# An FFT-and-maxout kernel: the first loads in one run, the table angles in two passes, and 35 table matmuls ahead of the work

## The chip, the cores and the metric

The kernel runs on one core of a Trainium2 chip. The metric is the device time of one execution in microseconds (us), the median of several runs. A core has a matrix engine (TensorE, PE in the profile; its weight loads are shown apart as PEld), three engines that work on vectors (VectorE or DVE, ScalarE or ACT, GpSimd or POOL) and SyncE (SP), which only issues transfers. Each works off its own list of instructions in the written order and waits on semaphores for the others. Transfers (DMAs) are issued by SyncE, ScalarE and GpSimd and carried out by 16 DMA engines that all share.

## The reference

```python
def _attn_ref(x):                      # x: 8 x 3072 x 256
    X = np.fft.fft(x, axis=1)
    X = np.fft.fft(X, axis=2)
    return X.real.astype(np.float32)

def _moe_ref(x, w1, w2, w3, w_out):    # x: 24576 x 256, d_ff = 768
    h = np.maximum(np.maximum(x @ w1, x @ w2), x @ w3)
    return (h @ w_out).astype(np.float32)
```

The output of the first goes into the second: the real part of a two-dimensional Fourier transform of each batch, then three projections, their maximum, and a projection back.

## The kernel before, in words

The transform along the sequence (3072 = 24 x 128) is done in two stages with matrices of sines and cosines, and the transform along the feature axis is folded into the weights, once, on the chip. The eight batches follow each other. A batch has two mixing stages: seven groups `s` (lines 421 to 442), small matmuls with the 24-point matrices `m24f`, `m24r`, `m0f`, `m0r`, whose results go to `z`; and six groups `k` (lines 444 to 462), which multiply `z` with the rows of the table `tab` into `t`. Then come 18 units of the feed-forward part (lines 470 to 502), into which the mixing of the next batch is woven by a plan written out by hand (lines 666 to 705). The schedule is manual: on each engine the instructions run in the order in which the program writes them.

The change lies in what happens before the first unit. That part consists of:

- Loads of batch 0. Rows 112 to 127 go to `xs_a` by SyncE and ScalarE (lines 165 and 166). The other 112 rows go to `x0_first` by sixteen transfers that GpSimd issues (lines 174, 182, 186, 187, all recorded at line 100), four for each run of 32 rows and four for the last 16. Between them GpSimd writes small index vectors: `i13` (line 172), `jm24` and `g24` (175 to 181), `dvec` (183 to 185). Behind them it issues the weight loads (191 to 198).
- The table. `tab` has 13 rows of 128 angles in three versions: sine, cosine and minus sine. `tab_angles` (233) takes three VectorE operations over all elements of the rows: angle in turns, rounding, remainder. `tab_sines` (246) takes three ScalarE passes: sine, absolute value, sine with a shift of a quarter turn (`half_pi`). `tab_minus` (254) is one VectorE operation. Rows 0 to 6 come first, then rows 7 to 12.
- The 24-point matrices (lines 262 to 302): some twenty small VectorE operations, one sine on ScalarE (292), and products on both.
- The rows of batch 0, turned and laid out: `turn_rows` and `lay_rows` (309 to 329, 346 to 355) copy each loaded run from (row, feature) into two arrays with the features outside, one of them reversed, on VectorE (`on_dve`) and ScalarE (`on_act`). The last strip is rows 95 to 111, split between the two engines by features.
- `md` and `nmd`, the 256-point matrix in two halves and its negative (lines 331 to 350): VectorE computes the angles `vm`, ScalarE takes the sine (345), VectorE derives the other half by alternating signs (349) and the negative (350). They multiply the weights in `prep_first` (367), which gives `gE`, `gO`, `gD`.
- The table matmuls (line 627), 27 matmuls on the finished table into a bank that nobody reads. They stand on TensorE ahead of the first `s` group.

Of the kernel before, what the change touches and what calls it, by code (L numbers as in the profile page):

```python
# [33 lines left out]
def kernel(  # L34
# [9 lines left out]
    nc = tc.nc  # L44
# [15 lines left out]
    consts = ctx.enter_context(tc.tile_pool(name="consts", bufs=1))  # L60
# [23 lines left out]
    gw = consts.tile([128, 768], BF16, tag="gw")  # L84
    rows_m = consts.tile([128, 12 * B], INT32, tag="rows_m")
    mark = consts.tile([1, 1], FP32, tag="mark")
    sgn = consts.tile([128, 1], FP32, tag="sgn")
    dif = consts.tile([128, 1], FP32, tag="dif")
    t_mid = consts.tile([128, 2, B], BF16, tag="t_mid")
# [6 lines left out]
    def load_rows(engs, dst, b, r0, r1, after=None):  # L96
        xr = x_rows(b)
        for g in range(4):
            eng = engs[g] if isinstance(engs, tuple) else engs
            ld = eng.dma_start(out=dst[g * 24:(g + 1) * 24], in_=xr[g, :, r0:r1, :])  # L100
            if after is not None:
                tc.add_manual_dep(ld.ins, after.ins.name, AFTER, reason="weights first")
# [50 lines left out]
    gen = gen_pool_cm.__enter__()  # L153
# [3 lines left out]
    def iota(t, pattern, base=0, cm=0):  # L157
        nc.gpsimd.iota(t, pattern, base=base, channel_multiplier=cm,
                       allow_small_or_imprecise_dtypes=True)
# [17 lines left out]
    iota(jm24[:, 13:24], [[-1, 11]], base=-1)  # L177
    iota(jm24[:, 24:37], [[1, 13]])
    iota(jm24[:, 37:48], [[1, 11]], base=1)
    g24 = gen.tile([96, 5], FP32, tag="g24")  # L180
    iota(g24, [[24, 5]])
    load_rows(nc.gpsimd, x0v[:, 32:64, :], 0, 32, 64)
    dvec = gen.tile([128, 128], FP32, tag="dvec")
    iota(dvec.rearrange("p (dl g) -> p dl g", g=4), [[1, 32], [64, 4]])
    iota(dvec[:, 2:4], [[64, 2]], base=32)
# [22 lines left out]
    nc.gpsimd.tensor_copy(rows_m, rows_f)  # L208

    consts_of = {}  # L210
    for (name, value) in (("half_pi", 0.5 * math.pi), ("rnd", ROUND), ("n24", -24.0)):
# [6 lines left out]
    half = gen.tile([128, 256], FP32, tag="half")  # L218
    nc.vector.memset(half[:, 0:128], 64.0)
    nc.vector.memset(half[:, 128:256], 0.0)  # L220
# [4 lines left out]
    nc.vector.tensor_scalar(out=pi13, in0=i13, scalar1=pidx, scalar2=1.0 / 3072.0,  # L225
                            op0=ALU.mult, op1=ALU.mult)

    w = gen.tile([128, 13 * 128], FP32, tag="w")
    v = gen.tile([128, 13 * 128], FP32, tag="v")
    q = gen.tile([128, 13 * 128], FP32, tag="q")  # L230
    turn = 2.0 * math.pi

    def tab_angles(r0, r1):
        cs = slice(r0 * 128, r1 * 128)
        n = r1 - r0
        nc.vector.scalar_tensor_tensor(
            out=v[:, cs].rearrange("p (r j) -> p r j", j=128),
            in0=j128.unsqueeze(1).to_broadcast([128, n, 128]), scalar=p128,
            in1=pi13[:, r0:r1].unsqueeze(2).to_broadcast([128, n, 128]),
            op0=ALU.mult, op1=ALU.add)  # L240
        nc.vector.tensor_scalar(out=q[:, cs], in0=v[:, cs], scalar1=ROUND, scalar2=None,
                                op0=ALU.add)
        nc.vector.scalar_tensor_tensor(out=w[:, cs], in0=q[:, cs], scalar=-ROUND, in1=v[:, cs],
                                       op0=ALU.add, op1=ALU.subtract)

    def tab_sines(r0, r1):
        cs = slice(r0 * 128, r1 * 128)
        wr = w[:, cs].rearrange("p (r j) -> p r j", j=128)
        nc.scalar.activation(out=tabs[:, r0:r1, 0, :], in_=wr, func=AX.Sin, scale=-turn)
        nc.scalar.activation(out=w[:, cs], in_=w[:, cs], func=AX.Abs)  # L250
        nc.scalar.activation(out=tabs[:, r0:r1, 1, :], in_=wr, func=AX.Sin, scale=-turn,
                             bias=consts_of["half_pi"])

    def tab_minus(r0, r1):
        nc.vector.tensor_scalar(out=tabs[:, r0:r1, 2, :], in0=tabs[:, r0:r1, 0, :],
                                scalar1=-1.0, scalar2=None, op0=ALU.mult)
# [52 lines left out]
    def turn_rows(copy, r0, n, d0, d1):  # L309
        reverse(copy, xr0, x0_first[:, r0 * 64:(r0 + n) * 64], r0, n, d0, d1)  # L310
# [4 lines left out]
    def lay_rows(copy, xs, r0, n, d0=0, d1=33):  # L315
        copy(out=xn0[:, d0:d1, r0:r0 + n],
             in_=bass.AP(xs.tensor, xs.offset + d0, [xs.ap[0], [1, d1 - d0], [64, n]]))

    def bf_rows(r0, n):
        return x0_first[:, r0 * 64:(r0 + n) * 64]  # L320
# [10 lines left out]
    turns = gen.tile([128, 256], BF16, tag="turns")  # L331
    nc.vector.memset(turns, 1.0)
    nc.vector.memset(turns.rearrange("p (q two g) -> p q two g", two=2, g=4)[:, :, 1, :], -1.0)
    vm = gen.tile([128, 256], FP32, tag="vm")
    qm = gen.tile([128, 256], FP32, tag="qm")
    nc.vector.scalar_tensor_tensor(
        out=vm.rearrange("p (k c) -> p k c", c=128),
        in0=dvec.unsqueeze(1).to_broadcast([128, 2, 128]), scalar=pidx,
        in1=half.rearrange("p (k c) -> p k c", c=128), op0=ALU.mult, op1=ALU.add)
    nc.vector.tensor_scalar(out=vm[:, 128:129], in0=pidx, scalar1=128.0, scalar2=64.0,  # L340
                            op0=ALU.mult, op1=ALU.add)
    nc.vector.tensor_scalar(out=qm, in0=vm, scalar1=256.0 * ROUND, scalar2=None, op0=ALU.add)
    nc.vector.scalar_tensor_tensor(out=vm, in0=qm, scalar=-256.0 * ROUND, in1=vm,
                                   op0=ALU.add, op1=ALU.subtract)
    nc.scalar.activation(out=md[0], in_=vm, func=AX.Sin, scale=float(-2.0 * math.pi / 256.0))
    turn_rows(on_act, 63, 32, 54, 65)
    turn_rows(on_dve, 63, 32, 32, 54)
    lay_rows(on_dve, bf_rows(64, 32), 64, 32)
    nc.vector.tensor_tensor(out=md[1], in0=md[0], in1=turns, op=ALU.mult)
    nc.vector.tensor_scalar(out=nmd_all, in0=md_all, scalar1=-1.0, scalar2=None, op0=ALU.mult)  # L350
    for (copy, a, b, c) in ((on_act, 49, 64, 17), (on_dve, 32, 49, 0)):
        turn_rows(copy, 95, 17, a, b)
        if copy is on_act:
            turn_rows(copy, 95, 16, 64, 65)
        lay_rows(copy, bf_rows(96, 16), 96, 16, c, c + 17 - c // 17)
    tab_minus(7, 13)
    nc.vector.tensor_scalar(out=sgn, in0=pidx, scalar1=0.0, scalar2=None, op0=ALU.is_equal)
    nc.vector.tensor_scalar(out=sgn, in0=sgn, scalar1=2.0, scalar2=-1.0,
                            op0=ALU.mult, op1=ALU.add)
# [263 lines left out]
                l2_queue.pop(0)  # L623

    warm = ps_s.tile([128, 512], FP32, name="warm", tag="ps")
    for _ in range(27):
        nc.tensor.matmul(warm, tab[:, 0:128], tab[:, 0:512], start=True, stop=True)
# [153 lines left out]
```

## Time and profile before

| | us |
|---|---|
| median of 3 runs | 425.91 (425.56 to 426.27) |
| the profiled execution | 424.57 |
| its span, first to last instruction | 422.8 |
| TensorE busy in the span | 404.0 (96%) |
| VectorE, ScalarE, GpSimd busy | 276.8, 258.9, 243.8 |

The profile is of one execution; its times are counted from the start of the span. The span plus 1.8 us around it is the execution's own time. In the rows of a list of instructions the first two numbers are start and length, then engine, line, operation, output, inputs, shape and count, and in brackets the idle time before it with what ended it. In rows of the chain of work there are start, length, engine, tile and line. A row may merge several instructions, and the ends of matmuls are modelled: they overlap, so the distance between starts tells the rate.

### The profile page before, as it was taken

What the parts mean: (1) busy time and instruction counts of PE and PEld (TensorE: products, weight loads), DVE (VectorE), ACT (ScalarE), POOL (GpSimd) and SP (SyncE); (2) the same over time, 40 slices, a digit from 0 to 9 for tenths busy, and PEclk for the clock granted to TensorE, in tenths of its full rate; (3) what the DMA queues carried; (4) which work ended last, traced back from release to release, by engine and by line L of the source; (5) the groups of instructions that cost most, each with busy time, mean ns of one, the idle gap of its engine ahead of it and who ended that gap; (6) DMA issues with size and microseconds to landing.
All of it is one profiled execution on the core that took longest, in us unless ns stands there. A gap on an engine that the chain in (4) does not pass through costs nothing.

```text
span 422.8 us, 8683 instructions
## 1 busy us (share of the span) xinstructions
PE 404.0 (96%) x3028; PEld 270.1 (64%) x3083; DVE 276.8 (65%) x460; ACT 258.9 (61%) x478; POOL 243.8 (58%) x291
## 2 busy tenths in 40 slices
PE   0899999999999999999999999999999999999996
PEld 0365667666676766666676666666666666666665
DVE  8877666566666665675666665675656665666773
ACT  6856666666665666556666666656665566655650
POOL 9927837962479526982299525983289621214420
PEclk9999999999999999999999999999999999999999
DMA  9998895793318831596217841387211221212213
GB/s 107 105 181 179 181 219 143 166 205 85 107 66 204 182 129 43 130 222 125 98 61 187 201 135 51 111 203 174 98 64 64 64 76 64 75 51 54 98 73 128
DMA packets 131172, 51.89 MB, mean 123 GB/s; under 512 B 113073, under 2 KB 128184, under 8 KB 131128
## 3 DMA queue, kind: packets, MB, share of 16 engines
q1 hardware_dynamic: 105408, 35.93, 35.8%
q0 software_dynamic: 24784, 15.08, 16.5%
q8 instruction: 24, 0.39, 0.4%
q10 hardware_dynamic: 936, 0.33, 0.3%
q14 instruction: 20, 0.16, 0.1%
HBM read 29.02 MB, written 25.17 MB: 128 GB/s over the span
## 4 chain that ended last, share of the span: by engine, by line
PE 87%; POOL 4%; DVE 3%; issue 3%; ACT 2%; DMA 1%; DVEq 0%; ACTq 0%; POOLq 0%
PE po L500 28%; PE pse L476 15%; PE pse L484 13%; PE pse L477 12%; PE po L524 4%; POOL x L100 3%; PE ps L458 2%; PE ps L456 2%; PE ps L430 2%; PE pl L516 2%; PE ps L432 2%; ACT stmp L490 1%; DVE ot L529 1%; PE psg L376 1%; DVE hp L491 1%
## 5 line engine op out<-in xcount | busy, mean ns | idle before, releaser
L490 ACT ACTIVATE stmp<-pse 128x512 bf16<-128x512 f32 x288 | 171.6, 600 | 52.0 <-PE pse L477 38.6
L534 POOL DMA_INDIRECT out_dram<-ot,rows_m x92 | 100.3, 1090 | 157.8 <-DVE ot L529 149.7
L491 DVE TENSOR_TENSOR hp<-pse,stmp 128x512 bf16<-128x512 f32 x144 | 99.6, 691 | 126.8 <-ACT stmp L490 87.0
L476 PE MATMUL pse<-t,gE 128*128 128x512 bf16 x285 | 108.1, 379 | 2.2 <-ACT t L460 0.2
L491 DVE TENSOR_TENSOR hm<-pse,stmp 128x512 bf16<-128x512 f32 x144 | 99.2, 689 | 6.8 <-ACT stmp L490 6.7
L477 PE MATMUL pse<-t,gO 128*128 128x512 bf16 x255 | 96.6, 379 | 0.2
L500 PE MATMUL po<-wout_bf,hp 128*128 128x256 bf16 x576 | 86.1, 273 | 0.3
L484 PE MATMUL pse<-t,gD 128*128 128x512 bf16 x274 | 82.7, 379 | 0.4
L500 PE MATMUL po<-wout_bf,hm 128*128 128x256 bf16 x570 | 77.8, 273 | 0.3
L500 PEld LDWEIGHTS <-hp 128*128 128x128 bf16 x576 | 56.3, 98 | 26.2
L500 PEld LDWEIGHTS <-hm 128*128 128x128 bf16 x576 | 56.4, 98 | 16.3
L144 POOL CAST x<-xs 96x1056 bf16<-96x1056 f32 x28 | 56.8, 2028 | 11.0 <-DMA xs<-in_x_dram 11.0
L529 DVE TENSOR_TENSOR ot<-po,even 128x512 f32<-128x512 f32 x92 | 62.9, 684 | 0.0
L146 POOL CAST x<-xs 96x1056 bf16<-96x1056 f32 (+1 forms) x35 | 58.2, 1675 | 0.0
L460 ACT CAST t<-ps 128x512 bf16<-128x512 f32 x47 | 27.5, 585 | 43.3 <-PE ps L458 43.2
L437 ACT CAST z_all<-ps 128x480 bf16<-128x480 f32 x45 | 25.1, 558 | 42.1 <-PE ps L432 42.1
L484 PEld LDWEIGHTS <-gD 128*128 128x128 bf16 x288 | 27.9, 98 | 32.2
L477 PEld LDWEIGHTS <-gO 128*128 128x128 bf16 x288 | 28.1, 98 | 20.3 <-issue 1.5
L476 PEld LDWEIGHTS <-gE 128*128 128x128 bf16 x288 | 28.1, 98 | 19.2 <-issue 0.4
L524 PE MATMUL po<-gw,t 128*128 128x512 bf16 x87 | 33.0, 379 | 0.0
L520 ACT COPY even<-pl 128x512 f32<-128x512 f32 x46 | 26.8, 582 | 0.1
L430 PE MATMUL ps<-m24f,x 96*128 96x96 bf16 x224 | 24.7, 205 | 0.0
(147 smaller groups left out, 328.2 us busy)
## 6 DMA issues: line engine op xcount, KB each, us to landing
xs<-in_x_dram SPq DMA_DIRECT2D x84, 198.0 KB
out_dram<-ot SPq DMA_DIRECT2D x90, 128.0 KB
xs<-in_x_dram SPq DMA_DIRECT2D x28, 192.0 KB
out_dram<-ot,rows_m POOLq DMA_INDIRECT x92, 3.3
x<-in_x_dram POOLq DMA_DIRECT2D x12, 96.0 KB, 4.3
w_bf<-in_moe_w_dram POOLq DMA_DIRECT2D x6, 192.0 KB, 5.5
out_dram<-ot SPq DMA_DIRECT2D x17, 64.0 KB
xs<-in_x_dram SPq DMA_DIRECT2D x32, 5.8 KB
```

What stands on the lines that cost most here:

```text
L144: nc.gpsimd.tensor_copy(v[:, 0:33, ch * 32:ch * 32 + 32], xs[:, 0:32 * 64].rearrange("p (bb dl) -> p dl bb", dl=64)[:, 0:33, :])
L146: reverse(lambda out, in_: nc.gpsimd.tensor_copy(out, in_), v[:, 33:66, :], xs, ch * 32, 33 if ch == 3 else 32)
L430: nc.tensor.matmul(ps1[:, c0:c0 + n], x0[0](d), mf[:, 0:n], start=True, stop=False)
L476: nc.tensor.matmul(pse[:, 0:n], gE[i][:, js], te, start=True, stop=False)
L477: nc.tensor.matmul(pse[:, 0:n], gO[i][:, js], to, start=False, stop=True)
L484: nc.tensor.matmul(pse, gD[i][:, js], to, start=False, stop=True, skip_group_check=True)
L490: nc.scalar.activation(out=stmp[:, 0:n], in_=pses[0][:, 0:n], func=AX.Relu)
L491: nc.vector.tensor_tensor(out=dst, in0=src3, in1=stmp[:, 0:n], op=ALU.max)
L500: nc.tensor.matmul(po, hcols(jc), wout_bf[:, jc * 256:(jc + 1) * 256], start=False, stop=(jc == NJC - 1), skip_group_check=True)
L524: nc.tensor.matmul(po, to[:, cp], gw[:, 256:768], start=True, stop=True)
L529: nc.vector.tensor_tensor(out=ot.rearrange("p (h c) -> p h c", h=2), in0=po.rearrange("p (h c) -> p h c", h=2), in1=lin.unsqueeze(1).to_br ...
L534: stored(nc.gpsimd.indirect_dma_start(out, bass.IndirectOffsetOnAxis(ap=rows_m[0:128 - lo, b * 12 + slot: b * 12 + slot + 1], axis=0), ot[ ...
```

## The change

The loads of batch 0 stand in one run. The index vectors that stood between them are either taken from `j128` (the vector 1 to 128) by VectorE or replaced by a slice of it:

```diff
-    i13 = gen.tile([128, 13], FP32, tag="i13")
-    iota(i13, [[1, 13]])
-    load_rows(nc.gpsimd, x0v[:, 0:32, :], 0, 0, 32)
-    jm24 = gen.tile([96, 48], FP32, tag="jm24")
-    iota(jm24[:, 0:13], [[1, 13]])
...
-    load_rows(nc.gpsimd, x0v[:, 64:96, :], 0, 64, 96)
+    for r0 in (0, 32, 64):
+        load_rows(nc.gpsimd, x0v[:, r0:r0 + 32, :], 0, r0, r0 + 32)
     load_rows(nc.gpsimd, x0v[:, 96:112, :], 0, 96, 112)
```

The angles take two passes over the elements instead of three. The part that depends on the column alone is reduced once on 128 elements (`step`), and two operations per piece remain. The pieces are rows 0 to 2, 3 to 6, 7 to 9 and 10 to 12; `w_late` holds the angles of the last piece:

```diff
+    nc.vector.tensor_scalar(out=step, in0=j128, scalar1=p128, scalar2=None, op0=ALU.mult)
+    nc.vector.tensor_scalar(out=near, in0=step, scalar1=ROUND, scalar2=None, op0=ALU.add)
+    nc.vector.scalar_tensor_tensor(out=step, in0=near, scalar=-ROUND, in1=step,
+                                   op0=ALU.add, op1=ALU.subtract)
...
     def tab_angles(r0, r1):
...
+        nc.vector.tensor_tensor(
+            out=wr.rearrange("p (r j) -> p r j", j=128),
+            in0=pi13[:, r0:r1].unsqueeze(2).to_broadcast([128, n, 128]),
+            in1=step.unsqueeze(1).to_broadcast([128, n, 128]), op=ALU.subtract)
+        nc.vector.scalar_tensor_tensor(out=wr, in0=wr, scalar=0.5, in1=wr,
+                                       op0=ALU.is_gt, op1=ALU.subtract)
...
-    tab_angles(0, 7)
-    tab_sines(0, 7)
-    tab_angles(7, 13)
-    tab_sines(7, 13)
+    for (r0, r1) in ((0, 3), (3, 7)):
+        tab_angles(r0, r1)
+        tab_sines(r0, r1)
+    jm24 = gen.tile([96, 48], FP32, tag="jm24")
```

Five small VectorE operations write `jm24` and `g24` at that place, and two write `dvec` further down. The angles of rows 7 to 12 and their sines stand between the copies of batch 0's rows, `vm` is computed by three operations instead of one, and its reduction moves behind the last strip, whose split between the engines moves from feature 49 to 54 and from 17 to 20:

```diff
     turn_rows(on_act, 0, 31, 32, 65)
+    tab_angles(7, 10)
+    tab_angles(10, 13)
+    lay_rows(on_act, bf_rows(0, 32), 0, 32)
+    tab_sines(7, 10, (0, 1))
     turn_rows(on_dve, 31, 32, 32, 65)
-    lay_rows(on_act, bf_rows(0, 32), 0, 32)
     lay_rows(on_dve, bf_rows(32, 32), 32, 32)
...
+    lay_rows(on_dve, bf_rows(64, 32), 64, 32)
+    tab_sines(7, 10, (2,))
+    tab_sines(10, 13, (0,))
+    for (copy, a, b, c, d) in ((on_dve, 32, 54, 0, 20), (on_act, 54, 64, 20, 33)):
+        turn_rows(copy, 95, 17, a, b)
```

There are 35 table matmuls. The sine of `md`, its sign copies and the last table passes stand among the `s` groups and behind them:

```diff
-    for _ in range(27):
+    for _ in range(35):
         nc.tensor.matmul(warm, tab[:, 0:128], tab[:, 0:512], start=True, stop=True)
...
+        if k == 2:
+            nc.scalar.activation(out=md[0], in_=vm, func=AX.Sin, scale=float(-2.0 * math.pi / 256.0))
+        if k == 3:
+            halves = [t.rearrange("p (q two g) -> p two q g", two=2, g=4) for t in md]
+            nc.vector.tensor_copy(out=halves[1][:, 0], in_=halves[0][:, 0])
+            nc.vector.tensor_scalar(out=halves[1][:, 1], in0=halves[0][:, 1], scalar1=-1.0,
+                                    scalar2=None, op0=ALU.mult)
+            nc.vector.tensor_scalar(out=nmd_all, in0=md_all, scalar1=-1.0, scalar2=None, op0=ALU.mult)
+    tab_sines(10, 13, (1, 2))
+    tab_minus(7, 13)
```

Nothing in the units themselves is changed, before or after.

More of the change, by code (lines that the diff above doesn't have):

```diff
@@ L86 @@
     mark = consts.tile([1, 1], FP32, tag="mark")
+    half_pi = consts.tile([128, 64], FP32, tag="half_pi")
+    w_late = consts.tile([128, 3 * 128], FP32, tag="w_late")
     sgn = consts.tile([128, 1], FP32, tag="sgn")
@@ L210 @@
     consts_of = {}
-    for (name, value) in (("half_pi", 0.5 * math.pi), ("rnd", ROUND), ("n24", -24.0)):
+    nc.vector.memset(half_pi[:, 0:1], 0.5 * math.pi)
+    for (name, value) in (("rnd", ROUND), ("n24", -24.0)):
         c = gen.tile([128, 1], FP32, name=name, tag=name)
@@ L224 @@
     pi13 = gen.tile([128, 13], FP32, tag="pi13")
-    nc.vector.tensor_scalar(out=pi13, in0=i13, scalar1=pidx, scalar2=1.0 / 3072.0,
+    nc.vector.tensor_scalar(out=pi13, in0=j128[:, 0:13], scalar1=pidx, scalar2=1.0 / 3072.0,
                             op0=ALU.mult, op1=ALU.mult)
-    w = gen.tile([128, 13 * 128], FP32, tag="w")
-    v = gen.tile([128, 13 * 128], FP32, tag="v")
-    q = gen.tile([128, 13 * 128], FP32, tag="q")
+    step = gen.tile([128, 128], FP32, tag="step")
+    near = gen.tile([128, 128], FP32, tag="near")
@@ L233, in tab_angles @@
     def tab_angles(r0, r1):
-        cs = slice(r0 * 128, r1 * 128)
+        wr = rows_of(r0, r1)
         n = r1 - r0
[L236 to L242, printed above, removed]
@@ new lines, in tab_angles, with tab_sines @@
+        nc.vector.scalar_tensor_tensor(out=wr, in0=wr, scalar=0.5, in1=wr,
+                                       op0=ALU.is_gt, op1=ALU.subtract)
+    def tab_sines(r0, r1, parts=(0, 1, 2)):
+        wf = rows_of(r0, r1)
+        wr = wf.rearrange("p (r j) -> p r j", j=128)
+        if 0 in parts:
+            nc.scalar.activation(out=tabs[:, r0:r1, 0, :], in_=wr, func=AX.Sin, scale=-turn)
+        if 1 in parts:
+            nc.scalar.activation(out=wf, in_=wf, func=AX.Abs)
+        if 2 in parts:
+            nc.scalar.activation(out=tabs[:, r0:r1, 1, :], in_=wr, func=AX.Sin, scale=-turn,
+                                 bias=half_pi[:, 0:1])
@@ L326 @@
     turn_rows(on_act, 0, 31, 32, 65)
+    tab_angles(7, 10)
+    tab_angles(10, 13)
+    lay_rows(on_act, bf_rows(0, 32), 0, 32)
+    tab_sines(7, 10, (0, 1))
     turn_rows(on_dve, 31, 32, 32, 65)
-    lay_rows(on_act, bf_rows(0, 32), 0, 32)
     lay_rows(on_dve, bf_rows(32, 32), 32, 32)
-    turns = gen.tile([128, 256], BF16, tag="turns")
-    nc.vector.memset(turns, 1.0)
-    nc.vector.memset(turns.rearrange("p (q two g) -> p q two g", two=2, g=4)[:, :, 1, :], -1.0)
+    dvec = gen.tile([128, 128], FP32, tag="dvec")
+    nc.vector.scalar_tensor_tensor(
+        out=dvec.rearrange("p (dl g) -> p dl g", g=4),
+        in0=j128[:, 0:4].unsqueeze(1).to_broadcast([128, 32, 4]), scalar=64.0,
+        in1=j128[:, 0:32].unsqueeze(2).to_broadcast([128, 32, 4]), op0=ALU.mult, op1=ALU.add)
+    nc.vector.tensor_scalar(out=dvec[:, 2:4], in0=j128[:, 0:2], scalar1=64.0, scalar2=32.0,
+                            op0=ALU.mult, op1=ALU.add)
     vm = gen.tile([128, 256], FP32, tag="vm")
     qm = gen.tile([128, 256], FP32, tag="qm")
[L336 to L339, printed above, removed]
+    nc.vector.tensor_scalar(out=vm[:, 0:128], in0=dvec, scalar1=pidx, scalar2=64.0,
+                            op0=ALU.mult, op1=ALU.add)
+    nc.vector.tensor_scalar(out=vm[:, 128:256], in0=dvec, scalar1=pidx, scalar2=None,
+                            op0=ALU.mult)
     nc.vector.tensor_scalar(out=vm[:, 128:129], in0=pidx, scalar1=128.0, scalar2=64.0,
                             op0=ALU.mult, op1=ALU.add)
+    turn_rows(on_act, 63, 32, 54, 65)
+    turn_rows(on_dve, 63, 32, 32, 54)
+    lay_rows(on_dve, bf_rows(64, 32), 64, 32)
[3 more added lines that the diff above has]
+        turn_rows(copy, 95, 17, a, b)
+        if copy is on_act:
+            turn_rows(copy, 95, 16, 64, 65)
+        lay_rows(copy, bf_rows(96, 16), 96, 16, c, d)
     nc.vector.tensor_scalar(out=qm, in0=vm, scalar1=256.0 * ROUND, scalar2=None, op0=ALU.add)
@@ L344 @@
                                    op0=ALU.add, op1=ALU.subtract)
[L345 to L356, printed above, removed]
     nc.vector.tensor_scalar(out=sgn, in0=pidx, scalar1=0.0, scalar2=None, op0=ALU.is_equal)
```

32 lines of the change are left out of this document (11 added, 21 removed).

## The prediction

> **What bounds the kernel now.** I read the span first, then the stretches of time, then the chain of work that ended last in the first 42 us.
>
> ```profile
> span 422.8 us, 8683 instructions
> ```
>
> ```profile
> 0.00:20.00 20.00, 8.25 (x27) 3.12 (x27) 17.65 (x54) 15.09 (x22) 18.99 (x35) 1.00 1.36 102
> ...
> 100.00:200.00 100.00, 99.24 (x762) 67.20 (x774) 64.05 (x99) 63.30 (x120) 60.87 (x67) 1.00 0.52 131
> ```
>
> The columns are the stretch, its length, the busy time and count of PE, PEld, DVE, ACT, POOL, then the clock, the DMA share and GB/s. From 20 us on TensorE is busy 99.2% of the time, and this change leaves that work alone. In the first 20 us TensorE does only 27 table matmuls (line 627) whose result nobody reads. So the change can move one thing: the moment T0 at which the real matmuls begin. What sets it is in the chain (start, length, what):
>
> ```profile
> 1.18 0.11 POOL i L158
> ...
> 5.08 0.48 POOL jm L158 x4
> 5.57 0.10 POOL g L158
> 5.66 3.20 POOL x L100 x4
> 8.86 0.43 POOL dvec L158
> ...
> 9.36 0.14 POOL dvec L158
> ...
> 9.59 6.50 POOL x L100 x7
> 16.08 2.77 DMA x<-in_x_dram
> ...
> 18.98 0.41 DVE back L131
> 19.39 0.60 DVE nat L316
> 20.12 0.20 PE ps L430
> ```
>
> T0 is 20.12. GpSimd works its instructions off one after another; the sixteen loads of batch 0 (L100) are among them, and the iotas i, jm, g and dvec stand between them. The last load is issued at 16.08, lands 2.77 later, and VectorE turns and lays its rows in 1.0 us. A second path ends almost at the same moment, the table matmuls:
>
> ```profile
> 11.72 8.25 PE L627 MATMUL warm<-tab 128*128 128x512 bf16 x27 [11.72 <-DVE tab L255]
> ```
>
> ```profile
> 15.52 0.15 PEld L627 LDWEIGHTS <-tab 128*128 128x128 bf16 x1 [0.28 <-issue]
> 15.94 0.15 PEld L627 LDWEIGHTS <-tab 128*128 128x128 bf16 x1 [0.28 <-issue]
> 16.35 3.12 PEld L627 LDWEIGHTS <-tab 128*128 128x128 bf16 x15 [0.26 <-issue]
> ```
>
> They start at 11.72, when L255 has written the table. Up to 16.35, eleven of them, they follow each other every 0.42 us; after that fifteen weight loads take 3.12 us, one per 0.216. So TensorE ran at half its rate for 4.6 us and then at full rate, and was free at 11.72 + 11 x 0.42 + 16 x 0.216 = 19.8, only 0.3 before the data. Both paths have to move for T0 to move.
>
> **Part 1, loads in one run.** The iotas i, jm, g and dvec leave the run. By the chain's rows: 0.11 + 0.48 + 0.10, and from 8.86 to 9.59 another 0.73, together 1.42; say 1.4. No other instruction of GpSimd is added; the weight loads behind move forward by the same 1.4, and so do batch 1's loads on SyncE, which wait for a weight load. The last landing goes from 16.08 + 2.77 = 18.85 to 17.45. Does VectorE slow the issuing? The single loads in the trace:
>
> ```profile
> L100 POOL DMA_DIRECT2D x<-in_x_dram x1: 834/834/834, 8.0 to 8.0; - x1
> ```
>
> ```profile
> L100 POOL DMA_DIRECT2D x<-in_x_dram x1: 1284/1284/1284, 11.2 to 11.2; - x1
> ```
>
> A load costs 0.83 us, but 1.28 where VectorE wrote bf16 tables and copies (from 11.16, below). VectorE does the same copies in the new order, still beside the last eight loads, so I leave this loss of about half a microsecond per touched load as it is. Bounds: a run wholly free of it would land another 0.8 earlier; two more touched loads would land it 0.9 later.
>
> **Part 2, the angles.** VectorE's rows:
>
> ```profile
> 1.70 1.15 DVE L236 SCALAR_TENSOR_TENSOR v<-j,p,pi 128x896 f32<-128x896 f32 x1
> ...
> 3.91 1.09 DVE L243 SCALAR_TENSOR_TENSOR w<-q,v 128x896 f32<-128x896 f32 x1
> ...
> 6.85 0.96 DVE L243 SCALAR_TENSOR_TENSOR w<-q,v 128x768 f32<-128x768 f32 x1
> 7.76 0.29 DVE L266 TENSOR_SCALAR ge<-g,pidx 96x5 f32<-96x5 f32 x1
> ...
> 11.16 0.41 DVE L255 TENSOR_SCALAR tab<-tab 128x896 bf16<-128x896 bf16 x1
> ...
> 12.26 1.11 DVE L131 COPY back<-x 96x1056 bf16<-96x1056 bf16 x1
> ...
> 15.87 0.43 DVE L343 SCALAR_TENSOR_TENSOR vm<-qm,vm 128x256 f32<-128x256 f32 x1
> 16.55 0.78 DVE L131 COPY back<-x 96x704 bf16<-96x704 bf16 x1 [0.25 <-DMA x<-in_x_dram]
> 17.25 1.08 DVE L316 COPY nat<-x 96x1056 bf16<-96x1056 bf16 x1
> ```
>
> Six long operations fill 1.70 to 7.76, 6.1 us. The new order has three operations on 128 elements (0.43 for 256 at 1.02 ns an element, which is (1.09 - 0.96) / 128, gives 0.3 each, 0.9), then two on 384 and two on 512 (1.09 less 0.52 and less 0.39: 0.57 and 0.70, 2.5 in all), and the five small operations that replace jm and g, 0.4 as an estimate from the spacing of this engine's short ones. That is 3.8, and two memsets ahead are gone (0.3). So L266 and all behind it start 6.1 - 3.8 + 0.3 = 2.6 earlier. ScalarE keeps up:
>
> ```profile
> 5.03 0.95 ACT L249 ACTIVATE tab<-w 128x896 bf16<-128x896 f32 x1 [2.02 <-DVE w L243]
> ...
> 10.52 0.27 ACT L292 ACTIVATE t<-v 96x96 f32<-96x96 f32 x1
> ...
> 18.95 0.76 ACT L131 COPY back<-x 96x255 bf16<-96x255 bf16 x2 [1.00 <-DMA x<-in_x_dram]
> ```
>
> Its three passes over seven table rows take about 3.2 us in two pieces from 3.5 on, over at 6.8, while the 24-point sine (10.52) is now due at 7.9. The table is then ready at 11.72 - 2.6 = 9.1. Thirty-five table matmuls from there, eleven at half rate: 9.1 + 11 x 0.42 + 24 x 0.216 = 18.9.
>
> The other six table rows are worked off later: four VectorE operations of 0.57 (2.3) and, before T0, four ScalarE passes of 0.95 x 384 / 896, about 0.45 (1.8). What hides them is the wait for the loads. ScalarE idles 1.0 before 18.95, loses md's sine, and all ahead of it begins 2.6 earlier: it is through near 16.8, against a landing at 17.45. VectorE had 7.2 from 11.16 to 18.33; 1.8 of that (14.5 to 16.3) goes, 2.3 and about 1.1 for dvec and vm come: 8.56 + 8.6 = 17.2. Spare 0.2; without this cover each 0.1 of VectorE's time costs 0.1.
>
> **Part 3, the last strip.** VectorE gets 22 and 20 rows of it where it had 17 and 17, 374 and 320 elements where it had 289 and 272. At (1.11 - 0.78) / 352 = 0.94 ns an element that is 0.13 more; ScalarE's share shrinks and ends beside it. T0 by data: 20.12 - 1.4 + 0.13 = 18.85; by the table matmuls 18.9. **T0 is near 19.0**, with the hand-over between the two, a gain of 1.1.
>
> **Part 4, md behind T0.** The 256-point sine moves behind the third eviction on ScalarE, its sign copies behind the fourth on VectorE, and two passes over table rows 10 to 12 behind the last.
>
> ```profile
> 18.26 0.27 DVE L349 TENSOR_TENSOR md_all<-md_all,turns 128x256 bf16<-128x256 bf16 x1
> 18.56 0.29 DVE L350 TENSOR_SCALAR nmd_all<-md_all 128x512 bf16<-128x512 bf16 x1
> ...
> 22.02 0.66 DVE L437 CAST z_all<-ps 128x480 bf16<-128x480 f32 x1 [0.19 <-PE ps L432]
> ```
>
> ```profile
> 16.85 0.41 ACT L345 ACTIVATE md_all<-vm 128x256 bf16<-128x256 f32 x1
> ...
> 21.59 0.56 ACT L437 CAST z_all<-ps 128x480 bf16<-128x480 f32 x1 [0.29 <-PE ps L432]
> ```
>
> ```profile
> 23.18 0.49 PE L376 MATMUL psg<-w_bf,nmd_all 128*128 128x384 bf16 x2
> ```
>
> In the clock of before: sine from 22.15 to 22.6, beside VectorE's eviction that ends at 22.68; two half copies 0.3, nmd 0.3: ready at 23.35 with the hand-overs, where TensorE wants it at 23.18. The third wait is new, 0.2 us, and everything behind it moves with TensorE; VectorE's next eviction, queued behind the copies, is 0.4 later, but TensorE needs it only after two groups of table-by-weight matmuls. Bounds: 0, if the copies overlap, and 0.6, if each half costs as much as the whole. The two late passes take 0.9 of ScalarE ahead of the next group's eviction, which becomes due about when they end: 0, at most 0.2. Moving vm behind the strip costs VectorE 0.8 before its first eviction, which is late only if that is over the second of spare there.
>
> **Sum.** 1.1 - 0.2 = 0.9 us off the span. The profiled execution took 424.57 (422.8 and 1.8 around it), so 423.7; the runs' median is 425.91, 1.3 above it, and the gain is carried over: **425.0**. This kernel's measurement can tell about 0.2% (0.85 us) from no change, so the forecast lies on that edge.
>
> **Rivals.** *(a) The clock decides.* T0 by the table matmuls is 9.1 + 35 x 0.216 + n x 0.204, n being those at half rate. Eleven were seen once; with 13 to 16, T0 is 19.3 to 19.9. For it: both paths are within 0.1 here. Against it: a single profile, which shows 11. Result 425.3 to 425.9, chance 0.17. The Trainium skill, "TensorE: Matmul & The Clock Gate", Part 1 (the HAM clock gate), says that the clock is raised after a busy window of 3.4 us that runs free of the kernel, so that one kernel may see 6, 11 or 14 cold matmuls. By that rule, the 11 of the trace are one draw, and the edge of this rival is as likely as the forecast's middle.
>
> *(b) Slower: the clock rises late.* Place: the table matmuls, eight more than before. From 21 of them at half rate on, T0 plus the md wait is over 0.85 later than before; all 35 would put T0 at 23.8, the result near 430. Against it: 4.6 us sufficed here. Chance 0.10, with all that would delay TensorE's start likewise.
>
> *(c) The loads land no earlier,* because moving the bytes, not issuing, limits them:
>
> ```profile
> DMA to landing us min/median/max: 2.8/4.2/5.3
> ```
>
> If so, T0 stays at 20.1 and md adds 0.2: 425.9 to 426.2. Against it: a load lands 2.8 to 5.3 after its issue and the last ones fastest, so no queue builds up. Chance 0.13.
>
> *(d) More than forecast:* md costs nothing and VectorE disturbs fewer loads, with a quick clock: 424.1 to 424.6, chance 0.15. The forecast's own range is 424.6 to 425.4, chance 0.45, some six tenths of it below 425.06. Faster thus gets 0.45, the same 0.45, slower 0.10; the range 424.1 to 426.1 leaves out (b) and the end of (c).
>
> **What would show it.** Sixteen loads of GpSimd without an iota between, the last landing near 17.4; the first table matmul near 9.1; T0 near 19.0; a wait of 0.2 ahead of nmd's first matmul; TensorE's waits beyond 30 us as before. Wrong would be a landing after 18, table matmuls that still run when the rows are laid, or a ScalarE pass between the landing and T0.

## The result, and the profile after

The kernel after takes **424.86 us** (median of 12 runs, 424.25 to 425.61), the kernel before in the same comparison 426.07 (424.95 to 426.39, 12 runs). The ratio is 0.9976, 95% interval 0.9967 to 0.9985: faster by 1.2 us, just over the 0.2% that can be told from no change. The forecast was 425.0.

The profiled execution of after took 424.95 with a span of 423.2, so its span is longer than that of before (422.8). But the profile of before is of a quick execution (424.57, under all twelve of the comparison), that of after of a middling one. The gain is therefore read at its place first, and the difference of the spans below. The stretches of time of after:

```profile
0.00:20.00 20.00, 10.68 (x66) 5.06 (x66) 17.30 (x63) 15.48 (x26) 19.06 (x29) 1.00 1.45 115
...
100.00:200.00 100.00, 98.17 (x753) 66.24 (x764) 62.69 (x98) 61.99 (x117) 60.87 (x67) 1.00 0.52 130
```

TensorE works 10.68 us of the first 20 instead of 8.25 and has 66 matmuls behind it instead of 27: the real work has begun inside this stretch. Between 100 and 200 us it works 98.17 instead of 99.24, which the end of this section takes up. The chain of work around T0, in start, length and what:

```profile
2.54 12.13 POOL x L102 x14
14.67 2.83 DMA x<-in_x_dram
17.59 0.60 ACT back L133 x2
18.20 0.45 ACT nat L318
18.73 0.20 PE ps L436
21.62 1.40 PE psg L382 x8
```

T0 is 18.73, against 20.12. The sixteen loads stand without an iota, the last is issued at 14.67 and lands at 17.50. The chain names ScalarE's half of the strip, but three paths end here within 0.65 us. TensorE's own list:

```profile
8.84 9.41 PE L633 MATMUL warm<-tab 128*128 128x512 bf16 x35 [8.84 <-DVE tab L249]
18.73 0.20 PE L436 MATMUL ps<-m24f,nat 96*128 96x96 bf16 x1 [0.48 <-ACT nat L318]
```

The 35 table matmuls run from 8.84 and leave TensorE free at 18.08: eight at half rate, 0.426 apart, and 27 at 0.216. (The row's own length has a modelled end, so its wait for the strip reads 0.48 only.) VectorE's list has no gap from 9.39 to T0:

```profile
9.39 1.27 DVE L133 CAST back<-xs 96x544 bf16<-96x544 f32 x2 [0.70 <-DMA xs<-in_x_dram]
...
12.36 1.09 DVE L133 COPY back<-x 96x1056 bf16<-96x1056 bf16 x1
...
17.62 0.48 DVE L133 COPY back<-x 96x374 bf16<-96x374 bf16 x1
18.02 0.56 DVE L318 COPY nat<-x 96x320 bf16<-96x320 bf16 x1
```

It reaches the strip at 17.62, 0.12 after the landing, and is done at 18.58. So landing, VectorE's list and table matmuls are all within reach of each other; the experiments have to tell which of them carries.

The gain of 1.39 at T0 is 1.30 a few microseconds later. Two rows of ScalarE show it, the first eviction of a unit, of before (27.10) and of after (25.80):

```profile
27.10 0.60 ACT L490 ACTIVATE stmp<-pse 128x512 bf16<-128x512 f32 x1
```

```profile
25.80 0.60 ACT L496 ACTIVATE stmp<-pse 128x512 bf16<-128x512 f32 x1
```

Where does it go by the end of the span? All waits of TensorE in after from 18 us on:

```profile
PE pse L482 <- ACT stmp L496: 0.7, 1, 0.7
PE ps L436 <- ACT nat L318: 0.5, 1, 0.5
PE pse L482 <- DVE hm L497: 0.5, 1, 0.5
PE pse L482 <- ACT t L466: 0.2, 1, 0.2
```

The first and the third, 1.2 in all, lie near 142 us. The same eviction of batch 1's mixing there, of before and of after:

```profile
139.41 0.56 ACT L437 CAST z_all<-ps 128x480 bf16<-128x480 f32 x1 [1.14 <-PE ps L432]
```

```profile
139.73 0.56 ACT L443 CAST z_all<-ps 128x480 bf16<-128x480 f32 x1 [2.77 <-PE pl L522]
```

ScalarE waited 2.77 us there instead of 1.14, and its lead of 1.3 had become a lag of 0.3. By the last operation of the chain the two kernels are level (419.36 and 419.37); the 0.4 by which the span of after is longer lies behind it. The change touches nothing there; what this hold is, the experiments only bound (last section).

### The profile page after: what moved, and what is told of

It is laid out like the page before. It is cut to its first block, busy times and chain, and to the rows that moved or that the text cites. A ratio compares the mean times of both kernels' runs of the same rounds, so it can differ in the third digit from the quotient of the medians.

```text
span 423.2 us, 8705 instructions
## 1 busy us (share of the span) xinstructions
PE 405.5 (96%) x3036; PEld 270.9 (64%) x3091; DVE 275.9 (65%) x469; ACT 259.4 (61%) x484; POOL 242.6 (57%) x283
## 4 chain that ended last, share of the span: by engine, by line
PE 87%; DVE 3%; POOL 3%; issue 3%; ACT 2%; DMA 1%; DVEq 0%; ACTq 0%; POOLq 0%
PE po L506 28%; PE pse L482 15%; PE pse L490 13%; PE pse L483 12%; PE po L530 4%; POOL x L102 3%; PE pl L522 2%; PE ps L464 2%; PE ps L462 2%; PE ps L436 2%; PE ps L438 2%; ACT stmp L496 2%; DVE ot L535 1%; PE psg L382 1%; DVE hp L497 1%
## 5 line engine op out<-in xcount | busy, mean ns | idle before, releaser
L506 PEld LDWEIGHTS <-hm 128*128 128x128 bf16 x576 | 56.4, 98 | 16.3
L482 PEld LDWEIGHTS <-gE 128*128 128x128 bf16 x288 | 28.1, 98 | 19.2 <-issue 0.4
```

Of the source, the lines that this page charges most:

```text
L482: nc.tensor.matmul(pse[:, 0:n], gE[i][:, js], te, start=True, stop=False)
L506: nc.tensor.matmul(po, hcols(jc), wout_bf[:, jc * 256:(jc + 1) * 256], start=False, stop=(jc == NJC - 1), skip_group_check=True)
```

## The experiments

The theory after the result: T0 carries the whole gain, and the last load's landing sets T0. Rivals: the eight more table matmuls do it by keeping the clock up; VectorE's list sets T0; the angles do it and not the loads; the loss near 140 us belongs to the program. All edits are made on the kernel after. Ratios are to the kernel before, on the same chip. The first four ran on a chip on which before takes 424.95, 1.1 less than in the result, so the times expected of them, written for the result's level, are to be read 1.1 lower.

**The index vectors back between the loads**, written to a tile that nothing reads.

```diff
+    iota(spare[:, 0:13], [[1, 13]])
+    load_rows(nc.gpsimd, x0v[:, 0:32, :], 0, 0, 32)
...
-    for r0 in (0, 32, 64):
-        load_rows(nc.gpsimd, x0v[:, r0:r0 + 32, :], 0, r0, r0 + 32)
```

> The changed kernel with GpSimd's index iotas back between the loads (they write a spare tile that nobody reads; 1.4 us by the rows of the kernel before). All else is as changed, the early table and the 35 table matmuls included. Theory (the last landing sets the start of the real matmuls, T0): the last load lands at 18.8 instead of 17.5, T0 goes from 18.73 to about 20.0, the whole gain is lost, 426.0 us. Rival (the earlier table is what bought the time): T0 moves by 0.3 at most, 424.9 to 425.2 us.

Measured: 424.59, ratio 0.9994 (0.9985 to 1.0002). The last load in the chain, VectorE's strip, and TensorE's first real matmul:

```profile
16.09 2.79 DMA x<-in_x_dram
```

```profile
19.00 0.47 DVE L133 COPY back<-x 96x374 bf16<-96x374 bf16 x1 [0.21 <-DMA x<-in_x_dram]
```

```profile
19.97 0.20 PE L446 MATMUL ps<-m24f,nat 96*128 96x96 bf16 x1 [1.66 <-DVE nat L328]
```

The last issue is back at 16.09 (before: 16.08), VectorE waits for its landing, T0 is at 19.97, and TensorE waits 1.66 although the 35 table matmuls begin only 0.5 later than in after (9.32). Without the run of loads the gain is gone: the 0.36 that is left can't be told from nothing.

**The loads without the angles**: after with the three passes over the angles of before, all 13 table rows ahead of the 24-point matrices, and 27 table matmuls. The run of loads, the new split of the strip and `md` behind T0 stay.

```diff
-    for (r0, r1) in ((0, 3), (3, 7)):
-        tab_angles(r0, r1)
-        tab_sines(r0, r1)
+    tab_angles(0, 7)
+    tab_sines(0, 7)
+    tab_angles(7, 13)
+    tab_sines(7, 13)
...
-    for _ in range(35):
+    for _ in range(27):
```

> The changed kernel with the three-pass angles of the kernel before, all 13 table rows ahead of the 24-point matrices, and 27 table matmuls; the loads stay in one run. Theory (two paths reach T0, both have to move): the last landing stays at 17.5, but the table is ready only near 11.7, and the 27 table matmuls end at 11.7 + 5.8 + 0.21 n for n of them at half rate, 19.2 to 20.9 with n from 8 to 16; T0 is set by them, 425.3 to 426.8 us. Rival (the loads alone bought the time): T0 near 18.8, 424.9 us.

Measured: 424.08, ratio 0.9981 (0.9972 to 0.9990).

```profile
11.15 8.55 PE L622 MATMUL warm<-tab 128*128 128x512 bf16 x27 [11.15 <-DVE tab L242]
19.54 0.21 PE L425 MATMUL ps<-m24f,nat 96*128 96x96 bf16 x1
```

The landing is at 17.59, and the table matmuls, which start late, hold T0 at 19.54, inside the theory's 19.2 to 20.9. The time, 0.87 under before, is 0.1 under the theory's range. By medians this has most of the gain, though its T0 is 0.8 behind after's; after itself was not run on this chip and the intervals of the two ratios overlap, so how much the angles add in time isn't settled by it. The trace gives them 0.8 at T0.

**27 and 50 table matmuls** instead of 35.

```diff
-    for _ in range(35):
+    for _ in range(27):
```

> The changed kernel with 27 table matmuls instead of 35, everything else as changed. Theory (the rows of batch 0 set T0): T0 stays at 18.7, TensorE idles some 2.2 us ahead of it instead of 0.5, the clock stays up over that pause, 424.9 us within 0.2. Rival (the eight more are needed to hold the clock): the first mixing groups run at half rate, 2.7 us become up to 5.4, 426 to 427.6 us.

> The changed kernel with 50 table matmuls instead of 35. Theory: fifteen more at full rate, 0.216 us each, are 3.2 us; T0 is then set by the table matmuls, 8.84 + 50 x 0.216 + 0.21 n, which is 21.3 with n = 8 at half rate and 23.0 with 16; 427.4 to 429.1 us, with a spread of the runs as wide as that of n. Rival (the end of the table matmuls does not hold up the real ones): no change, 424.9 us.

With 27: 424.95 (423.20 to 427.38 in 12 runs), ratio 0.9993 (0.9976 to 1.0011). With 50: 427.0 (426.61 to 428.41 in 5 runs), ratio 1.0058 (1.0045 to 1.0071). TensorE's list with 27, and the stretch behind T0 (the clock is the number before the last two):

```profile
18.72 0.20 PE L436 MATMUL ps<-m24f,nat 96*128 96x96 bf16 x1 [2.06 <-ACT nat L318]
...
19.39 0.28 PE L436 MATMUL ps<-m24f,nat 96*128 96x96 bf16 x1
19.47 0.28 PE L438 MATMUL ps<-m24r,back 96*128 96x96 bf16 x1
```

```profile
19.40:22.80 3.40, 3.40 (x47) 3.40 (x45) 2.06 (x7) 1.82 (x4) 2.56 (x7) 0.50 1.17 162
```

T0 is the same 18.72: the data sets it, not the number of table matmuls. But the wait of 2.06 ahead of T0 costs the clock: from 19.39 on the matmuls follow each other every 0.08 us instead of 0.04, for 3.4 us. Its twelve runs fall in two heaps, 423.2 to 423.8 (five, clock granted over the whole run 0.998 to 1.0) and 424.9 to 427.4 (seven, 0.991 to 0.996); the profiled one, 425.2, is of the second. The middles of the heaps, 423.31 and 425.11, lie 1.8 apart, and 3.4 us at half rate are 1.7 us of lost work. So the rival holds in part of the runs: the eight more don't make the gain, they protect it. Where the clock stays up, 27 are between 1.2 and 1.8 under before; whether that is better than 35, no run on this chip shows. With 50 the table matmuls set T0, at 21.25:

```profile
21.25 0.21 PE L436 MATMUL ps<-m24f,nat 96*128 96x96 bf16 x1
```

**The kernel after again**, in two more comparisons on two chips.

> The changed kernel itself, once more, beside the kernel before on the same chip. Its first profile held ScalarE for 1.3 us at 138 to 140 us, where the kernel before was not held, so that both spans came out alike though T0 was 1.4 us earlier. Theory (the hold is an accident of that execution): the profile shows T0 near 18.7 and no hold at that place, a span near 421.5; the median lies 1.0 to 1.5 us under that of before. Rival (the hold belongs to the changed program): ScalarE waits again near 138 us, a span of 423.

> The kernel after, unchanged, beside e9 to e11 on the same chip. Theory: 0.9976 of the kernel before, within the interval 0.9967 to 0.9985 of the first result, T0 18.7 to 18.9. Rival (the place of the 0.6% to 1% of spread is the chip): outside of that interval.

First: 425.02 against 426.15, ratio 0.9972 (0.9961 to 0.9983). Second: 424.61 against 425.52, ratio 0.9978 (0.9969 to 0.9987). The gain is the same 0.9 to 1.2 on each; the level moves with the chip by as much. T0 is 18.86 and 18.70. In the first it is TensorE that is late: VectorE and ScalarE are done with the strip at 18.37, and the table matmuls run without a gap into the real ones. In the second VectorE's list and the table matmuls end together (18.54, and 18.58 by the modelled end).

```profile
8.84 10.18 PE L633 MATMUL warm<-tab 128*128 128x512 bf16 x35 [8.84 <-DVE tab L249]
18.86 0.21 PE L436 MATMUL ps<-m24f,nat 96*128 96x96 bf16 x1
```

The hold near 140 us recurs in both, with TensorE's two waits on `stmp` and `hm`; so it is no accident of one execution, which the first one's theory held it to be, and the span is 423.3 instead of 421.5. The second shows how little one path is worth by itself: its loads were issued quicker and the last landed at about 16.7, 0.8 ahead of the result's profile, but VectorE's list came to the strip no earlier, and T0 stayed.

```profile
17.74 0.47 DVE L133 COPY back<-x 96x374 bf16<-96x374 bf16 x1
```

**VectorE's two bf16 copies of rows 31 to 63 as operations with two inputs** (the maximum of a tile with itself), beside which GpSimd's loads had taken longer.

```diff
+    on_two = lambda out, in_: nc.vector.tensor_tensor(out=out, in0=in_, in1=in_, op=ALU.max)
-    turn_rows(on_dve, 31, 32, 32, 65)
-    lay_rows(on_dve, bf_rows(32, 32), 32, 32)
+    turn_rows(on_two, 31, 32, 32, 65)
+    lay_rows(on_two, bf_rows(32, 32), 32, 32)
```

> The changed kernel with VectorE's two copies of rows 31 to 63 written as the maximum of a tile with itself (an operation of two inputs, same elements, same result) instead of a copy. Theory (a bf16 copy on VectorE holds up GpSimd's issuing): the fourteenth and fifteenth load take 0.70 us instead of 1.56 and 1.04, the last lands near 16.3 instead of 17.5; T0 stays within 0.2 of 18.7, because VectorE works without a pause up to the last strip; the time stays the same within 0.3 us. Rival (the queue of transfers holds up the issuing): the two loads stay long and the last landing at 17.5.

Measured: 428.51, ratio 1.0047 (1.0032 to 1.0063). GpSimd's loads in after, then here, and VectorE's list here:

```profile
1.47 13.88 POOL L102 DMA_DIRECT2D x<-in_x_dram  x16 [0.29 <-issue]
```

```profile
1.47 12.68 POOL L102 DMA_DIRECT2D x<-in_x_dram  x16 [0.29 <-issue]
```

```profile
12.19 2.25 DVE L333 TENSOR_TENSOR back<-x 96x1056 bf16<-96x1056 bf16 x1 [0.50 <-DMA x<-in_x_dram]
14.34 2.28 DVE L333 TENSOR_TENSOR nat<-x 96x1056 bf16<-96x1056 bf16 x1
```

The loads take 1.2 us less than in the result's profile and 0.7 to 1.2 less than in the profiles of after, so the copies did cost that, and the last load landed near 16.3, as expected. But a copy takes 2.25 instead of 1.09, which the theory had not reckoned with; VectorE comes to the strip at 20.00, and T0 is 20.95. Here VectorE's list sets T0, and an earlier landing is worth nothing. Of the 3.5 us over after on the same chip (425.02), 2.1 are T0; behind it TensorE ran at half rate for 3.4 us, and the first eviction of a unit is 3.6 later (29.51 for 25.93). The Trainium skill, "SBUF — State Buffer", section "SBUF: two separate sides", says that some VectorE operations lock GpSimd out of writing the descriptors of its transfers, so that a load is held until they end. The trace agrees that the copies hold the loads, by 0.7 to 1.2 us for 2.2 us of copies; that it is the descriptors, no row here shows.

**md before T0**: the reduction of `vm`, the sine, the two half copies and `nmd` stand ahead of the strip, as in before.

```diff
+    nc.scalar.activation(out=md[0], in_=vm, func=AX.Sin, scale=float(-2.0 * math.pi / 256.0))
...
-        if k == 2:
-            nc.scalar.activation(out=md[0], in_=vm, func=AX.Sin, scale=float(-2.0 * math.pi / 256.0))
```

> The changed kernel with the reduction of vm, the sine of md, its sign copies and nmd ahead of the last strip, as in the kernel before, instead of among the first mixing groups. Theory (VectorE has no time to spare ahead of T0): 0.7 us of vm and 0.6 of copies and nmd come before the strip, T0 goes from 18.7 to 19.6 or 20.0, and the wait of 0.1 us ahead of nmd's first matmul goes; 0.8 to 1.2 us slower than the changed kernel. Rival (the wait for the loads hides it): T0 unmoved, 0.1 us faster.

Measured: 425.68, ratio 0.9991 (0.9981 to 1.0001), 0.66 above the same chip's 425.02, a little under the 0.8 to 1.2 expected.

```profile
18.82 0.55 DVE L133 COPY back<-x 96x374 bf16<-96x374 bf16 x1
```

```profile
19.85 0.20 PE L442 MATMUL ps<-m24f,nat 96*128 96x96 bf16 x1 [1.25 <-DVE sgn L369]
```

VectorE has 1.4 us more ahead of the strip and comes to it at 18.82 instead of 17.34. T0 goes from 18.86, where the table matmuls were last, to 19.85. Its list has no spare. The time moves less than T0, since TensorE's two waits near 140 us are 0.7 here instead of 1.2.

**The last three table rows behind T0**, first with the 13 base angles in a small lasting tile, then in one of 64 numbers.

```diff
-    tab_angles(10, 13)
...
+    at(0, 3, lambda: tab_minus(10, 13))
-    pi13 = gen.tile([128, 13], FP32, tag="pi13")
+    pi13 = consts.tile([128, 13], FP32, tag="pi13")
```

> The changed kernel with the angles and the first sine of table rows 10 to 12 taken out of the time before T0: two VectorE operations (1.1 us) among the first table-by-weight groups, three ScalarE passes and the negation in the first units. Theory (two things end together before T0, the last landing at 17.5 and VectorE's own list): T0 stays at 18.6 to 18.7, VectorE now waits about 1 us for the last landing, the time stays the same within 0.3 us. Rival (VectorE's list alone sets T0): T0 near 17.9, limited by the 35 table matmuls at 18.1, 0.6 us faster.

> The kernel after with the angles and sines of table rows 10 to 12 moved from VectorE's and ScalarE's lists ahead of T0 to behind it, as in e8, but the 13 base angles lie in a tile of 64 numbers a row, so no later tile changes its place by a number of bytes that isn't a multiple of 256. VectorE's list is 1.2 us shorter. Theory (e8's 6 us came from where the tiles lie, which slowed the loads' packets): the loads issue and land as in the kernel after (last landing near 17.5), the result within 0.2% of the kernel after. Theory on T0 (the landing sets it): VectorE waits about 1 us for the last load and T0 stays near 18.6. Rival (VectorE's list sets T0, the landing is early enough): T0 falls to 17.9 to 18.1, where the table matmuls end. Rival on e8 (the late order itself slows the loads): fourth load lands after 12 and the result is near 431 again.

First form: 431.46, ratio 1.0132 (1.0107 to 1.0156), against all expectations. Second form: 425.13, ratio 0.9994 (0.9983 to 1.0005). The two forms have the same order of work and differ in that tile alone (and in the chip, of which after shows 0.4), so the 6 us were not the order of the work. In the second form VectorE's list is 1.2 shorter and T0 did not move:

```profile
12.28 1.09 DVE L133 COPY back<-x 96x1056 bf16<-96x1056 bf16 x1 [1.69 <-DMA x<-in_x_dram]
...
17.72 0.47 DVE L133 COPY back<-x 96x374 bf16<-96x374 bf16 x1
18.11 0.68 DVE L321 COPY nat<-x 96x320 bf16<-96x320 bf16 x1
```

VectorE stood idle 1.69 until rows 32 to 63 landed (12.26), worked from there on with one more gap of 0.44, came to the strip at 17.72, 0.4 after the last load had landed (17.3), and was done at 18.79. T0 was 18.93. So the last landing did not set it, as the theory had it, nor did T0 fall, as the rival had it: the work saved stood ahead of 12.28, where VectorE then waited for an earlier load, and its list behind that load ended last. Work taken from ahead of that landing is worth nothing; work put behind it, as `md` above, costs. The result is worse by 0.5 than after on the same chip; the two intervals just overlap. TensorE's one long wait in it, at 38.26, is for VectorE, whose list has no gap from the moved negation on:

```profile
PE pse L483 <- DVE hm L498: 1.2, 1, 1.2
```

```profile
34.82 1.60 DVE L252 TENSOR_SCALAR tab<-tab 128x384 bf16<-128x384 bf16 x1
```

**52 bytes**: after with a tile of 13 FP32 numbers a row among the lasting tiles, which nothing reads.

```diff
+    shift = consts.tile([128, 13], FP32, tag="shift")
...
+    nc.vector.memset(shift, 0.0)
```

> The kernel after with one more tile of 13 FP32 numbers a row (52 bytes), filled once and read by nothing, among the lasting tiles, so that all that is placed behind it lies 52 bytes further on. Theory (the place of the tiles costs e8's 6 us): 430 to 432, the fourth load of batch 0 lands near 12.5 instead of 9.2, GpSimd waits between loads. Rival (e8's loss came from the order of the work): within 0.2% of the kernel after, near 425.

Measured: 433.52 (2 runs, 431.26 and 435.78), ratio 1.0188 (1.0143 to 1.0233). The loads' queue between 2 and 14 us, of after, then here (packets, MB, the time of the packets as a share of the engines' time, over 100% where packets overlap):

```profile
q0 software_dynamic: 12511, 1.21, 170.1%
```

```profile
q0 software_dynamic: 9660, 0.93, 284.5%
```

Fewer packets take far more time: 170.1 over 12511 against 284.5 over 9660 is 2.2 times as long for one. GpSimd then waits for earlier loads before it can issue the next:

```profile
10.50 0.81 POOL L103 DMA_DIRECT2D x<-in_x_dram  x1 [0.95 <-DMA x<-in_x_dram]
12.06 3.43 POOL L103 DMA_DIRECT2D x<-in_x_dram  x4 [0.75 <-DMA x<-in_x_dram]
```

A tile that does nothing costs over 6 us: by the spans 429.5 against 422.8 on the same chip. T0 is 22.64, 3.9 later; behind it TensorE runs at half rate for 3.4 us, and further on it waits 1.7 us for rows that GpSimd converts. The first form above has its small tile among the lasting ones too, and lost its 6 us when that was padded. Which of the tiles behind it is the one that minds, and why, was not tried. An odd size alone is not the cause: after has lasting tiles of 104 and of 4 bytes a row (`m0f`, `sgn`) without the loss.

**Rows 96 to 111 by SyncE**, as FP32, in place of GpSimd's last four loads; the strip is turned ahead of rows 64 to 95, on top of the form above, with 30 table matmuls.

```diff
+    load_rows(nc.sync, xs_b.rearrange("p (bb dl) -> p bb dl", dl=64), 0, 96, 112)
-    load_rows(nc.gpsimd, x0v[:, 96:112, :], 0, 96, 112)
```

> e9, and rows 96 to 111 are loaded as FP32 by SyncE's queue, which is idle by then, instead of by GpSimd's last four loads; VectorE and ScalarE turn and lay this strip ahead of rows 64 to 95, and 30 table matmuls instead of 35. GpSimd's last landing is then of its twelfth load, near 15. Theory (the last landing set T0): T0 falls from 18.7 to 17.6 to 17.9, result about 0.9 us under the kernel after (ratio to the kernel before near 0.9955). Rival (the two queues share what moves the bytes, so that GpSimd's loads land as late as before): T0 stays above 18.5, no gain over the kernel after. Rival (30 table matmuls leave TensorE idle long enough for its clock to fall): half-rate matmuls behind T0, result 0.5 to 1.5 above the theory's in part of the runs.

Measured: 433.44 (428.47 to 433.89 in 6 runs), ratio 1.0147 (1.0106 to 1.0188): the rivals, both, and 8.8 over after. The first row of VectorE's copies of rows 31 to 63, and the queues between 2 and 14 us:

```profile
15.64 1.10 DVE L133 COPY back<-x 96x1056 bf16<-96x1056 bf16 x1 [4.97 <-DMA x<-in_x_dram]
```

```profile
q0 software_dynamic: 9731, 0.95, 136.5%
q1 hardware_dynamic: 2422, 0.60, 28.4%
```

The second queue moved 0.60 MB instead of 0.21, and GpSimd's moved 0.95 instead of 1.21 in the same time. Rows 32 to 63, which VectorE wants first, landed 3.4 later than in the form without this edit (15.65 instead of 12.26), T0 went to 21.89, and after its long wait TensorE ran at half rate (0.08 between starts) for 4.7 us. The first unit is 5.2 us later than in after; the rest of the loss comes later, a wait of TensorE of 2.0 for VectorE among it, and was not followed up. Transfers that look free take their time from the loads that are needed sooner.

## Why the prediction was right, by its steps

**T0 carries the change: shown.** With the index vectors back between the loads (T0 19.97) the gain is gone, with table matmuls until 21.25 the kernel is slower than before, and all three comparisons of after give the gain, with T0 from 18.70 to 18.86. The last landing alone, as the theory had it, does not set T0: last are ScalarE's half of the strip in one profile of after, the table matmuls in another, and the table matmuls and VectorE's list together in the third.

**Part 1, loads in one run, 1.4 earlier: right.** The last load was issued at 14.67 for 16.08 and landed at 17.50, where 17.45 was forecast. That VectorE's copies would still cost the issue "about half a microsecond per touched load" held in sum: the form without them is 0.7 to 1.2 quicker.

**Part 2: right in size, its spare too generous.** The table matmuls began at 8.84 (forecast 9.1). Eight at half rate gave 18.08 in the result's profile, twelve held T0 at 18.86 in another, so the draw of the clock that rival (a) priced decides which path is last, but only over some 0.2 us, since the data ends there as well. The sum for VectorE has a slip: 7.2 less 1.8, plus 2.3 and 1.1, is 8.8 and not 8.6, which leaves a spare of 0.1 and not 0.2. VectorE reached the strip 0.12 after the landing. Moving 1.4 us of work back ahead of the strip made VectorE 1.5 later there, as "each 0.1 of VectorE's time costs 0.1" says, and T0 1.0 later. One of the prediction's signs of being wrong, table matmuls that still run when the rows are laid, did come in the second of after's three profiles; it cost some 0.4. The Trainium skill, "TensorE: Matmul & The Clock Gate", Part 1 (the HAM clock gate), has the number of cold matmuls vary from run to run; the profiles of after show 8, 10 and 12, which agrees.

**Part 3, the strip, 0.13: within what can be read.** VectorE's share took 0.96 from 17.62 to 18.58, ScalarE's 1.06; both are behind the landing by one microsecond, as before.

**Part 4, md's wait, 0.2: right to 0.1.** The weight load for `nmd` waited for it:

```profile
PEld L382 <- DVE nmd_all L646: 0.2, 1, 0.2
```

and the first group of table-by-weight matmuls took 1.40 in the chain where the later ones take 1.30. The lead fell from 1.39 to 1.30 there. The late passes cost nothing that can be seen there.

**The sum**, 1.1 - 0.2 = 0.9, came out as 1.39 - 0.1 = 1.3 in the trace and 1.2 by the medians (0.9 and 1.1 in the other comparisons). The mis-sized term is T0: 19.0 was forecast, with the table matmuls taken as last at 18.9 and a hand-over on top; they ended at 18.08, and the two paths overlapped instead of adding. That 425.0 and 424.86 lie so close is partly luck: the gain was 0.3 larger than forecast, and before, from which it is taken off, was 0.16 slower in this comparison (426.07 instead of 425.91). "TensorE's waits beyond 30 us as before" was wrong, by 1.2 near 142 us.

**The rivals.** (a) did not come: it needed 13 or more at half rate, and after's profiles have 8, 10 and 12, a draw worth 0.2. The clock can take the whole gain, as with 27 table matmuls, but by a pause ahead of T0, which the prediction did not name. (b) wasn't seen: no profile had more than thirteen table matmuls at half rate. (c) is false for the end of the run, where the landing followed the issue; but the two last experiments show that the bytes do limit the loads before 14 us, so "no queue builds up" was wrong as a reason. (d) has the T0 that came, but not the time; of its reasons the quick clock was there in the result's profile, while VectorE did disturb the loads, and md's wait was there.

## What to carry to other kernels

Where three paths end together, a change has to move all of them, and each part taken alone shows less than its share: measure by undoing one part at a time, and look at the moment itself in the trace, not at the span. Shortening an engine's list helps only behind the load that it last waits for. Filler work that only keeps a clock up has a narrow best count: eight fewer lost the gain in seven runs of twelve, fifteen more made TensorE itself the bound. After any change of tiles compare the time per packet of the first transfers before believing anything else: 52 bytes cost more than five times what the change gained.

## What the runs showed of the hardware that was not expected

- The place of a tile: a shift of 52 bytes made a packet of the loads take 2.2 times as long, 6 us and more in all.
- In the profiles a pause of TensorE of 2.1 to 4.4 us ahead of T0 (to the modelled end of the table matmuls) was followed by half rate: for 3.4 us with 27 table matmuls, two-input copies, 52 bytes and the first late form, and for 4.7 us with SyncE's strip, where the granted clock had fallen 2 us before T0. Pauses of 1.25 and 1.66 were not. With 27 table matmuls it goes by runs: the granted clock is lower in seven of twelve.
- Two bf16 copies of VectorE beside GpSimd's loads lengthen their issue by 0.7 to 1.2 us in all; as operations with two inputs they don't, but take 2.25 each instead of 1.09. In the other direction, in the second late form, VectorE's negation of 384 elements, 0.28 us long at 22.50, took 1.60 at 34.82, while GpSimd was converting rows:

```profile
34.23 2.04 POOL L148 CAST x<-xs 96x1056 bf16<-96x1056 f32 x1
```

- The hold near 140 us: it is in all three of after's profiles, at the same eviction, and takes the lead down to 0 in the first, to less than 0 in the second, and to 0.4 in the third. It goes with the chip and not with one program: the six edited kernels on the chips of the two later comparisons have it too, whatever their T0, with ScalarE's wait at that eviction 1.93 to 2.65. The four edited kernels on the first chip don't have it, among them after with 27 table matmuls, nor has the profile of before:

```profile
139.59 0.56 ACT L443 CAST z_all<-ps 128x480 bf16<-128x480 f32 x1 [1.14 <-PE ps L438]
```

GpSimd issues an indirect store of 2.55 us at that time, in before and in all the others, so the store alone doesn't make the hold:

```profile
139.99 2.55 POOL L534 DMA_INDIRECT out_dram<-ot,rows_m  x1 [0.23 <-issue]
```

That the kernel before meets the hold as well on those chips would explain why the medians keep the gain that the spans don't show; it has one profile only, so this stays open.
